# Turning q and k of batches 1 to 3 by one crossbar DMA per batch in place of TensorE transposes

## The chip, the cores and the metric

The kernel runs on one core of a Trainium2 chip. The metric is device time in microseconds. Three timed runs of the kernel before gave 316.80, 317.67 and 317.11 us, a median of 317.11 us. One profiled execution took 317.23 us; its span, from the first to the last instruction in the trace, is 315.4 us. All readings of the trace are in microseconds from the start of that span.

## The reference, cut to what matters

Attention over 4 batches, 8 heads, 768 positions and head size 64 with a block mask, followed by a gated feed-forward over the 3072 tokens:

```
scores = (q @ k.T) / 8                      # per batch and head, 768 x 768
mask   = block mask of 24 x 24 blocks of 32 # window, first/last blocks, 3 random ones per row
attn   = softmax(where(mask, scores, -1e9))
x      = (attn @ v), heads side by side     # 3072 x 512
gate   = sigmoid(x @ w_gate)                # 512 -> 1536
out    = (gate * (x @ w_val)) @ w_out       # 1536 -> 512, float32
```

For the score product TensorE needs q and k with the head dimension on the partitions. They come from memory with the positions on the partitions, so each has to be transposed. That transposition is what the change moves.

## The kernel before, in words

**Units.** The work is cut into 12 units of 256 query positions, three per batch: units 0 to 2 are batch 0, units 3 to 5 batch 1, units 6 to 8 batch 2, units 9 to 11 batch 3. A unit has four head pairs, and a pair has three steps of 256 key positions each. A step is a group of 8 score matmuls (line 381), one exponential of 128x1024 on ScalarE (line 391) and one product with the mask on VectorE (line 397). The pair's products are then multiplied with v by 24 matmuls (line 420), normed on VectorE (lines 430 and 432) and transposed by two TensorE instructions (line 441).

**Feed-forward.** Each unit's feed-forward runs under the attention of the next units: 12 groups of 8 matmuls (line 505, with the tanh at line 516 and the gating at line 521), then two output groups of 12 matmuls (line 544), whose results are copied to `ysb` (four buffers) and stored by a DMA on SP's queue (line 562). The output groups of unit n stand in unit n + 2.

**Preps.** `prep` (line 318) turns q or k of one head pair of one batch. VectorE copies two heads side by side into `pr` (line 326), TensorE transposes six 128x128 blocks of it into a PSUM bank (line 335), and ScalarE or VectorE copies the bank to `qT` or `kT` (lines 222 and 224). There are 8 such preps for each of batches 1, 2 and 3. `vcopy` (line 359) copies v of a pair beside a column of ones. `q16`, `k16`, `v16`, `vex`, `qT` and `kT` each have two buffers, one for even and one for odd batches.

**Loads.** All loads go through POOL's queue in program order (line 175 for q, k and v, lines 185 and 190 for the weights) and convert float32 to float16. Those of batch 1 stand at the end of the start-up list; those of batches 2 and 3 wait until the buffer of the batch before the last has been copied (`later`, line 592).

**Order.** `Plan` (line 54) simulates the engines with a table of costs, hands each free engine the first ready task in program order, and the resulting order is then written out, engine by engine. On the chip every engine runs its own list in that order, and an instruction that waits holds up all that stands behind it on its engine.

Of the kernel before, what the change touches and what calls it, by code (L numbers as in the profile page):

```python
# [13 lines left out]
f16 = mybir.dt.float16  # L14
# [6 lines left out]
B, H, S, D = 4, 8, 768, 64  # L21
BLK = 32
NB = S // BLK
NT = S // 128
NP = H // 2
# [6 lines left out]
NU = S // UQ  # L32
PE, ACT, DVE, DMA = "PE", "ACT", "DVE", "DMA"
# [20 lines left out]
class Plan:  # L54
# [7 lines left out]
        self.tasks = []  # L62
        self.room = {kind: [(0.0, i) for i in range(n)] for kind, n in banks.items()}

    def add(self, engines, fn, deps=(), at=0.0, take=(), free=()):
        self.tasks.append((engines, fn, list(deps), at, list(take), list(free)))
        return len(self.tasks) - 1

    def run(self):
        n = len(self.tasks)  # L70
        left = [len(set(t[2])) for t in self.tasks]
        after = [[] for _ in range(n)]
        for i, t in enumerate(self.tasks):
            for d in set(t[2]):
                after[d].append(i)
        ready = sorted(i for i in range(n) if not left[i])
        busy = {PE: 0.0, ACT: 0.0, DVE: 0.0, DMA: 0.0}
        events = [(0.0, -1)] + [(t[3], -1) for t in self.tasks if t[3] > 0]
        heapq.heapify(events)
        order, end = [], 0.0  # L80
        while events:
            now, i = heapq.heappop(events)
            if i >= 0:
                for bank in self.tasks[i][5]:
                    self.room[bank.kind].append((now, bank.slot))
                for j in after[i]:
                    left[j] -= 1
                    if not left[j]:
                        bisect.insort(ready, j)
            if events and events[0][0] <= now:  # L90
                continue
            for eng in busy:
                if busy[eng] > now:
                    continue
                for j in ready:
                    engines, fn, _, at, take, _ = self.tasks[j]
# [12 lines left out]
                    heapq.heappush(events, (now + cost, -1))  # L109
                    heapq.heappush(events, (now + cost + self.LAG[eng], j))  # L110
# [10 lines left out]
def kernel(  # L121
# [11 lines left out]
    nc = tc.nc  # L133
# [6 lines left out]
            name=nc.get_next_instruction_name(), act_func_set_id=_set_id  # L140
# [11 lines left out]
    sing = ctx.enter_context(tc.tile_pool(name="sing", bufs=1))  # L152
# [12 lines left out]
    wo = sing.tile([128, NF, DM], f16)  # L165
    q16 = [sing.tile([128, H, NT, D], f16, name=f"q16_{r}") for r in range(2)]
    k16 = [sing.tile([128, H, NT, D], f16, name=f"k16_{r}") for r in range(2)]
    v16 = [sing.tile([128, H, NT, D], f16, name=f"v16_{r}") for r in range(2)]
    vex = [sing.tile([128, H, NT, D + 1], f16, name=f"vex{r}") for r in range(2)]
    qT = [sing.tile([128, NP, S], f16, name=f"qT{r}") for r in range(2)]  # L170
    kT = [sing.tile([128, NP, S], f16, name=f"kT{r}") for r in range(2)]


    def load_heads(dst, src, b, h0, h1, t0=0, t1=NT):
        nc.gpsimd.dma_start(  # L175
            dst[b % 2][:, h0:h1, t0:t1, :],
            src[b, h0:h1].rearrange("h (p t) d -> p h t d", t=NT)[:, :, t0:t1, :],
        )
# [79 lines left out]
    land = {}  # L258
# [59 lines left out]
    def prep(src, dst, b, p, t0, t1, deps, at):  # L318
# [35 lines left out]
            [(DVE, 0.14 + 0.07 * n), (ACT, 0.18 + 0.1 * n)], evac, [c] + deps, free=[bank]  # L354
        )

    def vcopy(b, p, deps, at):
        def go(eng):
            nc.vector.tensor_copy(
                vex[b % 2][:, 2 * p : 2 * p + 2, :, 0:D],  # L360
                v16[b % 2][:, 2 * p : 2 * p + 2, :, :],
            )

        a = plan.add([(DVE, 0.36)], go, loaded[b] + deps, at=at)
        copies[b].append(a)
        return a
# [37 lines left out]
    class Pair:  # L404
# [34 lines left out]
        def turn(self, eng):  # L439
            for s in range(2):  # L440
                nc.tensor.transpose(  # L441
                    m16(self.bank2.slot)[:, s * 128 : (s + 1) * 128],
                    self.x16[:, s, :, :],
                    ident,
                )
# [25 lines left out]
    def scores(run):  # L471


        def mm(eng):
            for pr, st in run:
                st.qk()

        deps = [x for pr, st in run for x in (kdone[pr.b, pr.p], qdone[pr.b, pr.p, pr.u])]
# [96 lines left out]
    xTs = [[] for _ in units]  # L575
    xdone = [[] for _ in units]
    ffn = [Ffn(n) for n in range(len(units))]
    masks, kdone, qdone, vdone, read = {}, {}, {}, {}, {}
    preps, valued, turned = deque(), deque(), deque()

    def prep_k(b, p, at=0.0):
        kdone[b, p] = prep(k16, kT, b, p, 0, NT, read.get(("qk", b - 2, p), []), at)

    def prep_q(b, p, at=0.0, t0=0, t1=NT):
        d_ = prep(q16, qT, b, p, t0, t1, read.get(("qk", b - 2, p), []), at)
        for u in range(t0 // 2, t1 // 2):
            qdone[b, p, u] = d_

    def prep_v(b, p, at=0.0):
        vdone[b, p] = vcopy(b, p, read.get(("pv", b - 2, p), []), at)  # L590

    def later(b):
        if b > 1:

            def load(eng):
                for src, dst in ((k, k16), (q, q16), (v, v16)):
                    load_heads(dst, src, b, 0, H)
# [109 lines left out]
```

## Time and profile before

| | |
|---|---|
| median of three runs | 317.11 us (316.80 to 317.67) |
| profiled execution | 317.23 us |
| its span | 315.4 us |
| TensorE busy | 299.3 us of the span |
| VectorE busy | 214.1 us |
| ScalarE busy | 214.1 us |
| transposes of preps (line 335) | 192 instructions, 17.1 us |

A timeline row gives the start, the duration, the engine, the line, the operation, the output and inputs with their shapes, and how many instructions were merged into the row; behind it, in brackets, stands the idle time before it and what ended that. A row by windows gives a stretch, its length, and the busy time of each engine with the number of instructions.

### The profile page before, as it was taken

Reading aid. Unit: us, or ns where it says so; the run is one execution under the profiler, and the core shown is the slowest. Engines: PE = TensorE matmul, PEld = TensorE weight load, DVE = VectorE, ACT = ScalarE, POOL = GpSimd, SP = SyncE. Lnnn points to the kernel's source line nnn. Section 1 sums busy time; section 2 is a strip of 40 time slices with the busy share of each in tenths; the row PEclk is TensorE's granted clock in tenths of the full one; section 3 lists DMA queues with packets and bytes.
Section 4 is the critical chain, followed back from the end, with each engine's and each line's share of the span. In section 5 each row is a group of like instructions: output and inputs, shape, how many; then the busy total and the mean of one; then the engine's idle time right before and its main releaser. Section 6 shows DMA issues by size and latency. Waiting matters only on the chain.

```text
span 315.4 us, 8130 instructions
## 1 busy us (share of the span) xinstructions
PE 299.3 (95%) x3470; PEld 217.6 (69%) x3470; DVE 214.1 (68%) x510; ACT 214.1 (68%) x344; POOL 25.9 (8%) x37
## 2 busy tenths in 40 slices
PE   2978999869999999999999999999999999999995
PEld 1355786658587688588588588588588588588682
DVE  4779878478577587688576578678577476577140
ACT  4679877737777677677778677677678678676341
POOL 8944301200000000000000000000000000000000
PEclk9999999999999999999999999999999999999999
DMA  7999999999100100100010100000000000100101
GB/s 101 179 201 203 207 204 204 234 202 150 67 3 2 69 2 1 69 2 2 33 36 2 59 10 3 35 33 2 35 35 1 35 35 3 55 14 2 67 2 67
DMA packets 23215, 21.03 MB, mean 67 GB/s; under 512 B 2164, under 2 KB 20108, under 8 KB 23180
## 3 DMA queue, kind: packets, MB, share of 16 engines
q0 software_dynamic: 19472, 14.16, 29.7%
q1 hardware_dynamic: 3708, 6.37, 5.5%
q8 instruction: 27, 0.44, 0.6%
q14 instruction: 8, 0.07, 0.1%
HBM read 28.39 MB, written 6.29 MB: 110 GB/s over the span
## 4 chain that ended last, share of the span: by engine, by line
PE 77%; DMA 19%; POOL 1%; DVE 1%; issue 1%; ACT 0%; POOLq 0%
PE m L505 36%; PE m L544 18%; DMA v<-in_v_dram 11%; PE m L420 10%; PE s L381 9%; DMA wo<-in_moe_w_out_dram 5%; DMA wv<-in_moe_w_val_dram 3%; PE m L335 2%; PE m L441 1%; POOL k L175 0%; POOL q L175 0%; DVE pt L397 0%; POOL v L175 0%; ACT ysb L555 0%; DVE x L432 0%
## 5 line engine op out<-in xcount | busy, mean ns | idle before, releaser
L391 ACT ACTIVATE pt<-s 128x1024 f16<-128x1024 f32 x144 | 140.2, 1027 | 7.0 <-PE s L381 6.3
L397 DVE TENSOR_TENSOR pt<-pt,mask 128x1024 f16<-128x1024 f16 x144 | 97.2, 686 | 31.0 <-ACT pt L391 30.7
L516 ACT ACTIVATE th<-m 128x256 f32<-128x256 f32 x144 | 55.1, 389 | 49.4 <-PE m L505 42.3
L505 PE MATMUL m<-xT,wg 128*128 128x256 f16 x576 | 86.7, 273 | 0.0
L505 PE MATMUL m<-xT,wv 128*128 128x256 f16 x576 | 86.4, 273 | 0.0
L521 DVE SCALAR_TENSOR_TENSOR ht<-th,m 128x256 f16<-128x256 f32 x144 | 56.9, 416 | 16.4 <-ACT th L516 15.2
L544 PE MATMUL m<-wo,ht 128*128 128x512 f16 x288 | 66.0, 379 | 0.0
L505 PEld LDWEIGHTS <-wv 128*128 128x128 f16 x576 | 56.4, 98 | 6.5
L505 PEld LDWEIGHTS <-wg 128*128 128x128 f16 x576 | 51.4, 98 | 11.1 <-issue 5.9
L420 PE MATMUL m<-vex,pt 128*128 128x65 f16 x1152 | 46.4, 196 | 3.6 <-DVE ht L521 1.8
L420 PEld LDWEIGHTS <-pt 128*128 128x128 f16 x1152 | 42.9, 99 | 8.9 <-issue 6.9
L544 PEld LDWEIGHTS <-ht 128*128 128x128 f16 x288 | 26.7, 98 | 30.5 <-issue 1.9
L381 PE MATMUL s<-qT,kT 64*128 64x256 f16 x576 | 46.9, 279 | 0.6 <-DVE qT L224 0.3
L555 ACT ACTIVATE ysb<-m 128x512 f32<-128x512 f32 x24 | 14.3, 597 | 35.2 <-PE m L544 35.2
L381 PEld LDWEIGHTS <-kT 64*128 64x128 f16 x576 | 22.0, 95 | 15.9 <-issue 8.6
L432 DVE TENSOR_TENSOR x<-m,rz 128x256 f16<-128x256 f32 x48 | 20.4, 424 | 1.7
L430 DVE RECIPROCAL rz<-m 128x4 f32<-128x4 f32 x48 | 8.7, 182 | 17.1 <-PE m L420 16.7
L335 PE MATMUL m<-ident,pr 128*128 128x128 f16 x192 | 17.1, 231 | 1.0 <-DVE kT L224 0.5
L224 DVE COPY xT<-m 128x256 f16<-128x256 f16 x32 | 9.3, 291 | 11.3 <-PE m L441 11.2
L335 PEld LDWEIGHTS <-pr 128*128 128x128 f16 x192 | 12.4, 103 | 5.5 <-issue 3.1
L441 PE MATMUL m<-ident,x 128*128 128x128 f16 x96 | 13.3, 221 | 1.5 <-DVE x L432 1.4
L441 PEld LDWEIGHTS <-x 128*128 128x128 f16 x96 | 9.0, 98 | 7.6 <-issue 1.6
(32 smaller groups left out, 87.1 us busy)
## 6 DMA issues: line engine op xcount, KB each, us to landing
out_dram<-ysb SPq DMA_DIRECT2D x24, 256.0 KB, 2.0
k<-in_k_dram POOLq DMA_DIRECT2D x3, 768.0 KB, 19.4
q<-in_q_dram POOLq DMA_DIRECT2D x3, 768.0 KB, 21.4
v<-in_v_dram POOLq DMA_DIRECT2D x3, 768.0 KB, 23.3
wg<-in_moe_w_gate_dram POOLq DMA_DIRECT2D x4, 384.0 KB, 12.6
wv<-in_moe_w_val_dram POOLq DMA_DIRECT2D x4, 384.0 KB, 13.5
wo<-in_moe_w_out_dram POOLq DMA_DIRECT2D x3, 512.0 KB, 16.5
k<-in_k_dram POOLq DMA_DIRECT2D x4, 192.0 KB, 5.5
```

Of the source, the lines that this page charges most:

```text
L335: nc.tensor.transpose(m16(bank.slot)[:, (t - t0) * 128 : (t - t0 + 1) * 128], box[0][:, t, :, :], ident,)
L381: nc.tensor.matmul(score[self.bank.slot][:, a, i, :], kT[b % 2][o : o + D, p, t * 128 : (t + 1) * 128], qT[b % 2][o : o + D, p, u * UQ : ( ...
L391: nc.scalar.activation(self.pt, score[self.bank.slot], AF.Exp, bias=0.0, scale=SCALE)
L397: nc.vector.tensor_tensor(self.pt, self.pt, m.unsqueeze(1).broadcast_to([128, 2, 2, UQ]), op=ALU.mult,)
L420: nc.tensor.matmul(self.acc[:, s, a, :], self.steps[t // 2].pt[:, a, t % 2, s * 128 : (s + 1) * 128], vex[self.b % 2][:, 2 * self.p + a, t ...
L432: nc.vector.tensor_tensor(self.x16, self.acc[:, :, :, 0:D], rz.broadcast_to([128, 2, 2, D]), op=ALU.mult,)
L441: nc.tensor.transpose(m16(self.bank2.slot)[:, s * 128 : (s + 1) * 128], self.x16[:, s, :, :], ident,)
L505: nc.tensor.matmul(pg[:, i, :], w[:, c, f * 128 : (f + 1) * 128], xTs[self.n][0][:, c, :], start=(c == 0), stop=(c == 3),)
L516: nc.scalar.activation(th, spare[bank.slot][:, 0:UQ], AF.Tanh, bias=0.0, scale=0.5)
L521: nc.vector.scalar_tensor_tensor(self.ht[:, f, :], in0=box[0], scalar=1.0, in1=spare[bank.slot][:, UQ : 2 * UQ], op0=ALU.add, op1=ALU.mult,)
L544: nc.tensor.matmul(spare[bank.slot], self.ht[:, f, s * 128 : (s + 1) * 128], wo[:, f, :], start=(f == 0), stop=(f == NF - 1),)
L555: nc.scalar.activation(ysb, spare[bank.slot], AF.Copy, bias=0.0, scale=0.5)
```

## The change

For batch 0 nothing changes. For batch 1 q and k are loaded as before, VectorE copies the head pairs side by side into two new tiles, `kp` and `qp`, which hold all four pairs of a batch (`pair_up`), and one transposing DMA on SP's queue writes all of `kT`, another one all of `qT` (`xbar`). For batches 2 and 3 the load itself writes the head pairs side by side: eight DMAs for k and eight for q, one per head, each with rows of 64 elements (`pair_load`). The transposing DMAs follow on SP's queue. `kp` and `qp` have one buffer each, so the load of batch 2 waits for the transposing DMAs of batch 1, and that of batch 3 for those of batch 2. A task can now have a delay of its own in `Plan` (`lag`), 10.0 for a transposing DMA and 55.0 for such a load; these are numbers of the order table.

```diff
+    qp = sing.tile([128, NP, NT, 2, D], f16, name="qp")
+    kp = sing.tile([128, NP, NT, 2, D], f16, name="kp")
...
+    def pair_up(src, dst, b, p, deps, at):
+        def go(eng):
+            nc.vector.tensor_copy(
+                dst[:, p, :, :, :],
+                src[b % 2][:, 2 * p : 2 * p + 2, :, :].rearrange("a h t d -> a t h d"),
+            )
+        return plan.add([(DVE, 0.36)], go, deps, at=at)
+
+    def xbar(src, dst, b, deps):
+        def go(eng):
+            nc.sync.dma_start_transpose(
+                dst[b % 2].rearrange("a p (t n) -> a (p t) n", n=128),
+                src.rearrange("a p t h d -> a (p t h d)"),
+            )
+        return plan.add([(DMA, 0.01)], go, deps, lag=10.0)
...
+    def pair_load(dst, src, b):
+        for p in range(NP):
+            for a in range(2):
+                nc.gpsimd.dma_start(
+                    dst[:, p, :, a, :],
+                    src[b, 2 * p + a].rearrange("(n t) d -> n t d", t=NT),
+                )
+
     def later(b):
-        if b > 1:
+        kr = [x for p in range(NP) for x in read.get(("qk", b - 2, p), [])]
+        if b == 1:
+            # for k, then q: four pair_up, then one xbar
...
+        else:
             def load(eng):
-                for src, dst in ((k, k16), (q, q16), (v, v16)):
-                    load_heads(dst, src, b, 0, H)
-            loaded[b].append(plan.add([(DMA, 0.01)], load, copies[b - 2]))
-        for p in range(NP):
-            for nm, fn in (("k", prep_k), ("q", prep_q), ("v", prep_v)):
-                preps.append(
-                    lambda fn=fn, p=p, at=land[nm, "next"] if b == 1 else 0.0: fn(b, p, at)
-                )
+                pair_load(kp, k, b)
+                pair_load(qp, q, b)
+                load_heads(v16, v, b, 0, H)
+            ld = plan.add(
+                [(DMA, 0.01)],
+                load,
+                [turned_b["k", b - 1], turned_b["q", b - 1]] + copies[b - 2],
+                lag=55.0,
+            )
+            loaded[b].append(ld)
+            turned_b["k", b] = xbar(kp, kT, b, [ld] + kr)
+            turned_b["q", b] = xbar(qp, qT, b, [ld] + kr)
...
+        for p in range(0, NP, 2):
+            at = land["v", "next"] if b == 1 else 0.0
+            preps.append(lambda p=p, at=at: [prep_v(b, p + i, at) for i in range(2)])
```

The change also moves instructions. On VectorE, in unit 2, where batch 1 is prepared (`k_1` and `q_1` are batch 1; `k_0`, `q_0` and `v_0` at this place are batch 2), there stood before, with the copies for batch 2 at the end:

```order
L326 COPY pr<-q_1_74 128x768
L359 COPY vex_80<-v_1_78 128x12x64 x2
L397 TENSOR_TENSOR pt<-pt,mask 128x1024
L224 COPY xT<-m_125 128x256
L359 COPY vex_80<-v_1_78 128x12x64 x2
L326 COPY pr<-k_0_75 128x768
L430 RECIPROCAL rz<-m_122 128x4
L432 TENSOR_TENSOR x_977<-m_122,rz 128x256
L397 TENSOR_TENSOR pt<-pt,mask 128x1024
L326 COPY pr<-q_0_73 128x768
L397 TENSOR_TENSOR pt<-pt,mask 128x1024
```

Now the same place reads as follows (line 422 is the mask product, 455 and 457 the norm, 384 the copy of v, 364 the new pairing copy):

```order
L364 COPY kp<-k_1_76 128x768 x4
L548 SCALAR_TENSOR_TENSOR ht<-th,m_124 128x256
L422 TENSOR_TENSOR pt<-pt,mask 128x1024 x2
L455 RECIPROCAL rz<-m_125 128x4
L457 TENSOR_TENSOR x_832<-m_125,rz 128x256
L364 COPY qp<-q_1_74 128x768 x4
L422 TENSOR_TENSOR pt<-pt,mask 128x1024 x2
L227 COPY xT<-m_127 128x256
L384 COPY vex_82<-v_1_80 128x12x64 x3
L455 RECIPROCAL rz<-m_125 128x4
L457 TENSOR_TENSOR x_922<-m_125,rz 128x256
L422 TENSOR_TENSOR pt<-pt,mask 128x1024 x2
```

The four k copies and the four q copies stand together, and no copy for batch 2 stands in unit 2 any more; the four copies of batch 2's v come 60 mask products into the program, those of batch 3's v 95 into it.

SP's queue had four small loads and then the 24 stores of the output. Now the transposing DMAs stand between the stores (`kT_86` and `qT_84` are the buffers of batches 1 and 3, `kT_85` and `qT_83` those of batch 2):

```order
L375 DMA_TRANSPOSE kT_86<-kp 128x24x128
L589 DMA out_dram<-ysb 128x512
L375 DMA_TRANSPOSE qT_84<-qp 128x24x128
L589 DMA out_dram<-ysb 128x512 x5
L375 DMA_TRANSPOSE kT_85<-kp 128x24x128
L375 DMA_TRANSPOSE qT_83<-qp 128x24x128
L589 DMA out_dram<-ysb 128x512 x6
L375 DMA_TRANSPOSE kT_86<-kp 128x24x128
L375 DMA_TRANSPOSE qT_84<-qp 128x24x128
L589 DMA out_dram<-ysb 128x512 x12
```

The q transposition of batch 1 stands behind the first store of unit 0, those of batch 2 behind the second store of unit 2, and those of batch 3 behind the second store of unit 5.

On POOL's queue the end of the list was one DMA each for k, q and v of batches 1, 2 and 3. For batches 2 and 3 there now stands:

```order
L622 DMA kp<-in_k_dram 128x6x64 x8
L622 DMA qp<-in_q_dram 128x6x64 x8
L178 DMA v_0_79<-in_v_dram 128x8x384
L622 DMA kp<-in_k_dram 128x6x64 x8
L622 DMA qp<-in_q_dram 128x6x64 x8
L178 DMA v_1_80<-in_v_dram 128x8x384
```

The load of v now stands behind sixteen smaller DMAs. On TensorE the 24 groups of six transposes of batches 1 to 3 are gone, and the other groups keep their places but for a neighbour here and there; the first score group of units 3, 6 and 9 is the first to read what a transposing DMA wrote.

More of the change, by code (lines that the diff above doesn't have):

```diff
@@ L63, in __init__, with add @@
         self.room = {kind: [(0.0, i) for i in range(n)] for kind, n in banks.items()}
-    def add(self, engines, fn, deps=(), at=0.0, take=(), free=()):
-        self.tasks.append((engines, fn, list(deps), at, list(take), list(free)))
+    def add(self, engines, fn, deps=(), at=0.0, take=(), free=(), lag=None):
+        self.tasks.append((engines, fn, list(deps), at, list(take), list(free), lag))
         return len(self.tasks) - 1
@@ L95, in run @@
                 for j in ready:
-                    engines, fn, _, at, take, _ = self.tasks[j]
+                    engines, fn, _, at, take, _, lag = self.tasks[j]
                     cost = dict(engines).get(eng)
@@ L109, in run @@
                     heapq.heappush(events, (now + cost, -1))
-                    heapq.heappush(events, (now + cost + self.LAG[eng], j))
+                    lag = self.LAG[eng] if lag is None else lag
+                    heapq.heappush(events, (now + cost + lag, j))
                     order.append((eng, fn))
@@ L476, in mm @@
                 st.qk()
-        deps = [x for pr, st in run for x in (kdone[pr.b, pr.p], qdone[pr.b, pr.p, pr.u])]
+        deps = [
+            x for pr, st in run for x in kdone[pr.b, pr.p] + qdone[pr.b, pr.p, pr.u]
+        ]
         a = plan.add([(PE, 0.1 + 0.22 * len(run))], mm, deps, take=[st.bank for pr, st in run])
@@ L577 @@
     ffn = [Ffn(n) for n in range(len(units))]
-    masks, kdone, qdone, vdone, read = {}, {}, {}, {}, {}
+    masks, kdone, qdone, vdone, read, turned_b = {}, {}, {}, {}, {}, {}
     preps, valued, turned = deque(), deque(), deque()
     def prep_k(b, p, at=0.0):
-        kdone[b, p] = prep(k16, kT, b, p, 0, NT, read.get(("qk", b - 2, p), []), at)
+        kdone[b, p] = [prep(k16, kT, b, p, 0, NT, [], at)]
     def prep_q(b, p, at=0.0, t0=0, t1=NT):
-        d_ = prep(q16, qT, b, p, t0, t1, read.get(("qk", b - 2, p), []), at)
+        d_ = [prep(q16, qT, b, p, t0, t1, [], at)]
         for u in range(t0 // 2, t1 // 2):
```

22 lines of the change are left out of this document (added).

## The prediction

> **What bounds the kernel now.** I read the page's busy times and slices first, then its chain, then TensorE's share of the preps.
>
> ```profile
> PE 299.3 (95%) x3470; PEld 217.6 (69%) x3470; DVE 214.1 (68%) x510; ACT 214.1 (68%) x344; POOL 25.9 (8%) x37
> ...
> PE   2978999869999999999999999999999999999995
> ...
> DMA  7999999999100100100010100000000000100101
> ...
> PE 77%; DMA 19%; POOL 1%; DVE 1%; issue 1%; ACT 0%; POOLq 0%
> ...
> L335 PE MATMUL m<-ident,pr 128*128 128x128 f16 x192 | 17.1, 231 | 1.0 <-DVE kT L224 0.5 <-DVE pr L326 0.4
> ```
>
> From about the tenth slice on TensorE is busy in nine tenths of each slice or more; before that the DMA engines are full, and the eighth and ninth slices (55 to 71 us) show TensorE at 8 and 6 tenths. So two things can be gained: TensorE work in the long dense stretch, and idle time around 60 us. VectorE and ScalarE at 68% bound nothing.
>
> A matmul's recorded 231 ns overlaps its neighbours, so it is no price. The price is what a prep adds to a unit. The view by windows, cut at the first score group of units 3 to 11 and limited to line 335, shows it (length, then TensorE busy and count; six are one prep):
>
> ```profile
> 76.54:99.96 23.42, 0.50 (x6) 0.38 (x6) 1.00 0.09 27
> 99.96:124.06 24.10, 1.52 (x18) 1.05 (x18) 1.00 0.07 23
> 124.06:148.50 24.44, 2.01 (x24) 1.43 (x24) 1.00 0.07 23
> 148.50:171.92 23.42, 0.50 (x6) 0.38 (x6) 1.00 0.07 24
> 171.92:196.02 24.10, 1.52 (x18) 1.05 (x18) 1.00 0.06 23
> 196.02:220.45 24.43, 2.01 (x24) 1.43 (x24) 1.00 0.06 23
> 220.45:243.54 23.09, 0.00 (x0) 0.00 (x0) 1.00 0.07 24
> 243.54:266.63 23.09, 0.00 (x0) 0.00 (x0) 1.00 0.07 25
> ```
>
> A unit without a prep takes 23.09 us; one prep makes it 23.42, three 24.10, four 24.44. That is 0.34 us per prep, very regular, hence TensorE time and nothing else.
>
> The idle time shows in the timeline of TensorE and VectorE, and in one row of the unrestricted windows:
>
> ```profile
> 48.36:76.54 28.18, 24.82 (x295) 18.62 (x292) 21.03 (x55) 17.67 (x29) 2.63 (x3) 1.00 1.30 211
> ...
> 48.36 0.83 PE L335 MATMUL m<-ident,pr 128*128 128x128 f16 x12
> ...
> 63.99 0.93 PE L420 MATMUL m<-vex,pt 128*128 128x65 f16 x24 [1.85 <-DVE ht L521]
> ...
> 68.07 0.27 PE L441 MATMUL m<-ident,x 128*128 128x128 f16 x2 [1.40 <-DVE x L432]
> ```
>
> ```profile
> 62.65 0.36 DVE L326 COPY pr<-q 128x768 f16<-128x768 f16 x1 [3.03 <-DMA q<-in_q_dram]
> ...
> 66.51 0.36 DVE L359 COPY vex<-v 128x768 f16<-128x768 f16 x1 [1.91 <-DMA v<-in_v_dram]
> ```
>
> VectorE stands at the copies of batch 2's q and v, which have not landed yet; mask products and gatings are queued behind them, and TensorE runs dry behind those: 28.18 - 24.82 = 3.36 us idle between the first prep of batch 1 (48.36) and the first score group of batch 1 (76.54).
>
> **The change part by part.**
>
> *Preps of batches 2 and 3, taken off TensorE.* The six windows from 76.54 to 220.45 hold 16 preps and last 143.91 us; six clean ones last 6 x 23.09 = 138.54. Gain: 5.37 us.
>
> *Preps of batch 1.* All 8 lie between 48.36 and 76.54. At 5.37 / 16 = 0.336 us each: 2.69 us.
>
> *The stall.* In unit 2 no copy waits for batch 2 any more, so what TensorE waited for at 63.99 and 68.07 is gone: 3.36 us. VectorE's next copies in the queue are those of batch 1's v, which the trace shows without a wait at 55.00 (row below). I count the whole 3.36.
>
> *VectorE and ScalarE* lose the copies into and out of the transposes. Since a clean unit already runs at TensorE's pace, that is worth nothing.
>
> *The new waits: when the transposing DMAs of batch 1 begin.*
>
> ```profile
> 47.21 0.62 DVE L326 COPY pr<-k 128x768 f16<-128x768 f16 x2
> ...
> 51.05 0.62 DVE L326 COPY pr<-q 128x768 f16<-128x768 f16 x2
> ...
> 55.00 0.63 DVE L359 COPY vex<-v 128x768 f16<-128x768 f16 x2
> ...
> 51.82 0.60 ACT L555 ACTIVATE ysb<-m 128x512 f32<-128x512 f32 x1 [1.72 <-PE m L544]
> ```
>
> k of batch 1 is copied at 47.21 with no wait ahead of it. Four copies in a row, two of which take 0.62, end at about 48.5, and the k transposition is issued. The q copies follow two mask products and a norm, near 51; they end about 52. The q transposition also stands behind the first store of unit 0, whose `ysb` (51.82 to 52.42) comes some 0.7 us sooner without the two preps ahead of it. So q is issued near 52.
>
> *When they are needed.* The first score group of unit 3 comes at 76.54 - 3.36 - 2.69 = 70.5. On one queue the second follows the first, so with T for one transposition both are there at 48.5 + 2T. The cover is 22.0 us and holds up to T = 11.0; beyond, TensorE waits 2T - 22.0.
>
> *What T is.* No row shows a transposing DMA. The nearest:
>
> ```profile
> q0 software_dynamic: 19472, 14.16, 29.7%
> q1 hardware_dynamic: 3708, 6.37, 5.5%
> ...
> out_dram<-ysb SPq DMA_DIRECT2D x24, 256.0 KB, 2.0
> ...
> ident<-bb_ident SPq DMA_DIRECT2D x1, 32.0 KB, 1.6
> ```
>
> It moves 768 KB in 24 x 128 = 3072 rows of 256 B. From below: SP's queue moved 6.37 MB in 5.5% of 315.4 us, 367 GB/s; 0.786 MB take 2.1 us, with the landing of the smallest row (1.6) 3.7 us. From above by packets: 3708 packets in 16 x 17.3 us are 75 ns each; 192 rows per engine make 14.4, with the landing 16.0 us. Far above: `ident` is one 128x128 block of rows of 256 B and lands in 1.6 us; were each of the 24 blocks such a transfer of its own, one behind the other, 38.4 us. It is one DMA with many rows, so the packet rows are nearest; between 3.7 and 16.0 I take 10. Then batch 1's last transposition is there at 68.5, 2 us ahead of its need, and costs nothing. The 38.4 stays for a rival.
>
> *The loads of batches 2 and 3.* Their 16 DMAs have 12,288 rows of 128 B in place of 2048 of 768 B.
>
> ```profile
> L175 POOL DMA_DIRECT2D k<-in_k_dram x7 | 5.7, 819 | 18.6 <-DVE qT L224 15.9 <-DVE pt L397 1.3 <-POOLq L691 0.8
> ...
> 40.00:50.00 10.00, 10.00 (x136) 8.06 (x132) 7.73 (x20) 8.55 (x15) 0.00 (x0) 1.00 1.31 204
> ...
> 108.05 0.33 SPq L562 DMA_DIRECT2D out_dram<-ysb  x1
> ...
> 180.01 0.33 SPq L562 DMA_DIRECT2D out_dram<-ysb  x1
> ...
> 122.98 0.68 DVE L397 TENSOR_TENSOR pt<-pt,mask 128x1024 f16<-128x1024 f16 x1
> ...
> 193.47 0.68 DVE L397 TENSOR_TENSOR pt<-pt,mask 128x1024 f16<-128x1024 f16 x1
> ```
>
> By bytes (1.57 MB at 204 GB/s) k and q take 7.7 us; by packets (POOL's queue spent 77 ns on each of its 19,472) 59 us; issuing 17 DMAs at 0.82 is 14 us. I take the middle of the ends, 33 us, and 3.9 for v. Batch 2: k starts when its buffer is free (58.5), v lands near 95. VectorE copies that v after 60 mask products, at 122.98 before, so at 122.98 - 6.05 - 4 x 0.336 = 115.6: 20 us of cover. Its transpositions stand behind the second store of unit 2 (108.05 before, near 101), end near 121, and are needed by unit 6 at 148.50 - 6.05 - 8 x 0.336 = 139.8: 18 us. Batch 3: `kp` is free at 111, v lands near 148; its copy stands after 95 mask products (193.47, less 9.7: 183.7). Its transpositions stand behind the second store of unit 5 (180.01, near 171), end near 191, needed by unit 9 at 209.0: 18 us. Stores queued behind a waiting transposition have four buffers, and the next one comes a whole unit later. So the loads cost nothing, and if all that cover is gone the price is in the rivals.
>
> **Sum.** 5.37 + 2.69 + 3.36 = 11.42 us. The profiled execution took 317.23 with a span of 315.4; less 11.42, span 304.0 and time 305.8. The median shown is 317.11, so execution and median agree to 0.12.
>
> **The rivals.**
>
> *Slower: the crossbar is slow.* If the 24 blocks go one by one, T is near `ident`'s 1.6 per block. Batch 1 waits 2T - 22.0; batches 2 and 3, from 101 to 139.8 and from 171 to 209, each wait 2T - 38. At T = 16.7 the first wait eats the whole gain, and from there on the change loses; T = 20 gives 305.8 + 18 + 2 + 2 = 328, T = 38.4 gives 305.8 + 54.8 + 38.8 + 38.8 = 438. For it: nothing in the trace excludes such a price. Against it: all other rows show the queues overlapping packets on 16 engines. Here the Trainium skill speaks against the change: "VectorE: DVE Perf Modes", section "The three transpose paths", gives 1309 ns for a 128x128 block by DMA against 390 ns on TensorE, and its rules advise TensorE where a PSUM destination will do. The trace disagrees on TensorE (0.336 us for six blocks, 56 ns each); for the DMA no run here shows it. By its figure T would be an estimated 31.4 us, and the time about 396 us.
>
> *Faster, but with a wait at unit 3.* T between 11.0 and 16.7: TensorE waits 0 to 11 us once, batches 2 and 3 are still covered. T = 14 gives 305.8 + 6 = 312.
>
> *The stall only moves.* Batch 1's v is loading until near 55 while the k transposition shares its DMA engines. If v comes several us later, VectorE stands at its copies as it stands at 62.65 now, and the 3.36 is not won: 309.2. Against it: TensorE has about 3 us of queued work that needs nothing behind those copies.
>
> *The small rows are slow.* At the full 77 ns per row batch 2's v lands at 58.5 + 59 + 3.9 = 121.4, 6 us after its copy is due, and batch 3's about when due: 305.8 + 6 = 312. The Trainium skill, "DMA: Bandwidth & Descriptors", section "Specifications", says that transfers under 512 B fall below line rate; no row here is as small as 128 B, and it gives no price.
>
> **How the numbers follow.** Forecast 0.56, wait at unit 3 0.17, slow crossbar 0.14, stall moved 0.08, slow rows 0.05. The forecast's own range is 303 to 308: the low end prices each of the 24 preps by the time that the chain of waits gives one (row below), 24 x 0.44 + 3.36 = 13.9 off; the high end leaves 2 us of wait.
>
> ```profile
> 141.01 0.44 PE m L335 x6
> ```
>
> The range to hold 8 in 10 goes up through the second, fourth and fifth case to T = 16.5: 303 to 317. What a measurement can tell from no change is 0.3%, about 1 us. Faster than that: the forecast and the three mild cases but for the last stretch of the second, 0.83; within it 0.03; slower 0.14.
>
> **What would show it.** Right: line 335 left with 48 transposes; every unit from 3 to 11 at 23.1 us; no idle time of TensorE over 1 us between 55 and 75; the transposing DMAs landing within 11 us, and no wait of a score group for one. Wrong: first score groups of units 3, 6 or 9 waiting for `kT` or `qT` (slow crossbar), VectorE waiting at copies of v, or units that stay above 23.4 with no prep in them.

## The result, and the profile after

The changed kernel takes 306.72 us, the median of four runs (305.60 to 307.56), against 316.96 us (316.80 to 317.67) for the kernel before in the same comparison: ratio 0.9671, 95% interval 0.9633 to 0.9708. (Ratios leave out a run that is over 1.5% above the fastest of its kernel.) The prediction was 305.8. The profiled execution took 306.27 us with a span of 304.5 (predicted 304.0).

The page of the kernel after, in the lines that were shown of the kernel before:

```profile
PE 291.4 (96%) x3326; PEld 209.6 (69%) x3326; DVE 200.9 (66%) x474; ACT 210.7 (69%) x340; POOL 48.5 (16%) x65
...
PE   3978999999999999999999999999999999999994
...
DMA  7999999999500699930100580100100100100101
...
q0 software_dynamic: 40400, 14.16, 40.8%
q1 hardware_dynamic: 22332, 11.09, 15.0%
...
PE 93%; ACT 2%; DMA 1%; DVE 1%; issue 1%; POOL 1%; POOLq 0%
```

TensorE has 144 instructions less, and the 8 and 6 of the eighth and ninth slices are 9 and 9 now. The share of DMA in the chain has gone from 19% to 1%. The loads and transposing DMAs of batches 2 and 3 stand as separate bursts (the digits over 1 behind the tenth slice), with low slices between them.

The same windows of the kernel after, unit 2 first, then units 3, 5, 6, 8 and 9, then from unit 11 to the end (length; TensorE, weight load, VectorE, ScalarE, POOL busy; granted clock; DMA share; GB/s):

```profile
47.23:70.33 23.10, 23.10 (x274) 16.89 (x274) 18.37 (x47) 17.06 (x28) 12.21 (x16) 1.00 1.59 184
70.33:93.42 23.09, 23.09 (x273) 16.97 (x273) 15.44 (x36) 16.80 (x27) 1.70 (x3) 1.00 0.58 75
...
116.51:139.61 23.10, 23.10 (x274) 16.98 (x274) 16.74 (x39) 17.08 (x28) 7.41 (x9) 1.00 1.04 104
139.61:162.70 23.09, 23.09 (x273) 16.96 (x274) 15.44 (x36) 16.80 (x27) 0.00 (x0) 1.00 0.07 24
...
185.79:208.89 23.10, 23.10 (x274) 16.88 (x274) 16.02 (x38) 17.06 (x28) 0.00 (x0) 1.00 0.07 24
208.89:231.98 23.09, 23.09 (x273) 16.97 (x273) 15.44 (x36) 16.80 (x27) 0.00 (x0) 1.00 0.07 24
...
255.07:304.50 49.43, 45.00 (x445) 32.06 (x444) 22.33 (x53) 24.18 (x44) 0.00 (x0) 0.98 0.09 33
```

Length and TensorE's busy time are the same number in every row but the last, which is the end of the program: no stall is left. Units 3, 6 and 9 begin at 70.33, 139.61 and 208.89 (predicted 70.5, 139.8 and 209.0).

The transposing DMAs of the kernel after, in SP's timeline around unit 2 (start, time for which the DMA held SP's queue):

```profile
48.60 6.18 SPq L375 DMA_TRANSPOSE kT<-kp  x1
54.83 0.58 SPq L589 DMA_DIRECT2D out_dram<-ysb  x1
55.46 3.85 SPq L375 DMA_TRANSPOSE qT<-qp  x1
```

And by tile, `kT` first and then `qT`, all three batches:

```profile
DMA to landing us min/median/max: 6.1/7.2/8.2
...
DMA to landing us min/median/max: 5.7/7.1/7.8
```

The longest of each, 8.2 and 7.8, are batch 1's. So k is there at 48.60 + 8.2 = 56.8 and q at 55.46 + 7.8 = 63.3, 7.1 us ahead of unit 3. SP is held for less time than a transposition takes, and the q one was issued 1.3 us before the k one had landed.

### The profile page after: what moved, and what is told of

Read it like the earlier page. It is cut to its first block, busy times and chain, and to the rows that moved or that the text cites. A ratio compares the mean times of both kernels' runs of the same rounds, so it can differ in the third digit from the quotient of the medians.

```text
span 304.5 us, 7858 instructions
## 1 busy us (share of the span) xinstructions
PE 291.4 (96%) x3326; PEld 209.6 (69%) x3326; DVE 200.9 (66%) x474; ACT 210.7 (69%) x340; POOL 48.5 (16%) x65
## 3 DMA queue, kind: packets, MB, share of 16 engines
q1 hardware_dynamic: 22332, 11.09, 15.0%
## 4 chain that ended last, share of the span: by engine, by line
PE 93%; ACT 2%; DMA 1%; DVE 1%; issue 1%; POOL 1%; POOLq 0%
PE m L532 42%; PE m L571 21%; PE s L406 13%; PE m L445 13%; PE m L466 2%; DMA v<-in_v_dram 1%; ACT pt L416 1%; PE m L303 1%; PE m L338 1%; ACT mask L225 1%; DVE pt L422 0%; DVE kT L227 0%; POOL k L178 0%; POOL q L178 0%; ACT ysb L582 0%
## 5 line engine op out<-in xcount | busy, mean ns | idle before, releaser
L548 DVE SCALAR_TENSOR_TENSOR ht<-th,m 128x256 f16<-128x256 f32 x144 | 57.3, 418 | 16.4 <-ACT th L543 14.8
L622 POOL DMA_DIRECT2D kp<-in_k_dram x16 | 13.0, 822 | 64.1 <-DMA kT<-kp 37.9
L622 POOL DMA_DIRECT2D qp<-in_q_dram x16 | 13.1, 827 | 0.7 <-DVE pt L422 0.4
```

The lines of the kernel that those rows point to most:

```text
L548: nc.vector.scalar_tensor_tensor(self.ht[:, f, :], in0=box[0], scalar=1.0, in1=spare[bank.slot][:, UQ : 2 * UQ], op0=ALU.add, op1=ALU.mult,)
L622: nc.gpsimd.dma_start(dst[:, p, :, a, :], src[b, 2 * p + a].rearrange("(n t) d -> n t d", t=NT),)
```

## Experiments

The theory is the prediction's sum: three terms that add, with the transposing DMAs hidden. The rivals that the result does not exclude by itself are that one term is larger than told and another smaller, and that the cover was there by luck. Four questions follow: do the terms stand alone (the first three), how far does the cover reach (the fourth), what sets the time of a transposition and of the loads (the fifth to tenth), and can it be beaten (the last two).

### The stall alone

In the kernel before, the order table's cost of a load is raised, so that the copies of batch 2 are put later. All transposes stay on TensorE.

```diff
-    LAG = {PE: 0.25, ACT: 0.06, DVE: 0.06, DMA: 16.0}
+    LAG = {PE: 0.25, ACT: 0.06, DVE: 0.06, DMA: 40.0}
```

> The kernel before with one number of the order table changed (the delay that the table gives a load, 40 in place of 16), so that no copy of batch 2 stands in unit 2 any more; all transposes stay on TensorE. Theory (the change gains 3.36 us by the stall and 8.06 us by TensorE time, each on its own): the idle time at 62 to 68 us goes, first score group of unit 3 at 73.2, time 317.0 - 3.4 = 313.6. Rival (the stall is only paid elsewhere, the whole gain is TensorE time): 317.0.

Measured: 313.09 us (312.22 to 313.92), ratio 0.9865 (0.9831 to 0.9899); span 312.1. Its windows, from the first prep of batch 1 to 73.00, just ahead of unit 3, and units 3 to 8:

```profile
48.36:73.00 24.64, 24.64 (x306) 18.97 (x303) 20.24 (x51) 18.10 (x29) 2.63 (x3) 1.00 1.30 213
73.23:217.15 143.92, 143.92 (x1730) 107.12 (x1730) 105.61 (x247) 102.39 (x164) 0.00 (x0) 1.00 0.10 28
```

TensorE is busy for the whole of the first stretch, and unit 3 begins 3.31 us sooner than before (73.23 against 76.54). Units 3 to 8 last 143.92, as before (143.91). The span lost 3.3 us. The stall is its own term, it was worth what the prediction gave it (3.36), and it could be had without the crossbar.

### Batches 2 and 3 by crossbar, batch 1 on TensorE

```diff
         if b == 1:
-            for nm, src, dst, dT, done in (
-                ("k", k16, kp, kT, kdone),
-                ("q", q16, qp, qT, qdone),
-            ):
...
+            for p in range(NP):
+                for nm, fn in (("k", prep_k), ("q", prep_q)):
...
+                        fn(b, p, land[nm, "next"])
```

> The change for batches 2 and 3 alone; batch 1 keeps its preps on TensorE. Theory: first score group of unit 3 at 73.2 (stall gone, 8 preps still there), units 3 to 8 at 23.1 each, time 306.7 + 2.7 = 309.4. Rival (batch 1's preps cost nothing, since TensorE has to wait in the start-up anyway): 306.7.

Measured: 309.40 us (308.94 to 309.75), ratio 0.9746 (0.9711 to 0.9780). Unit 2, with the 8 preps of batch 1 in it, and unit 3:

```profile
48.09:73.87 25.78, 25.78 (x322) 19.66 (x322) 20.50 (x51) 19.46 (x32) 9.43 (x11) 1.00 1.43 143
73.87:96.96 23.09, 23.09 (x273) 16.97 (x273) 15.41 (x36) 16.80 (x27) 0.00 (x0) 1.00 0.07 24
```

25.78 - 23.10 = 2.68 us for 8 preps (predicted 2.69), and no idle time. Unit 3 begins at 73.87, 0.7 us later than was expected; unit 2 had begun 0.86 us later than in the change. The kernel is 2.7 us behind the change.

### Batch 1 by crossbar, batches 2 and 3 as before

The copies of batch 2 were kept late as in the first experiment, so that only the preps of batch 1 and the stall should be gone.

```diff
-    LAG = {PE: 0.25, ACT: 0.06, DVE: 0.06, DMA: 16.0}
+    LAG = {PE: 0.25, ACT: 0.06, DVE: 0.06, DMA: 40.0}
...
-                pair_load(kp, k, b)
-                pair_load(qp, q, b)
-                load_heads(v16, v, b, 0, H)
+                for src, dst in ((k, k16), (q, q16), (v, v16)):
+                    load_heads(dst, src, b, 0, H)
...
+                for fn in (prep_k, prep_q, prep_v):
+                    preps.append(lambda fn=fn, p=p: fn(b, p, 0.0))
```

> The change for batch 1 alone; batches 2 and 3 keep their loads and their preps on TensorE, with their copies standing late in the order (delay 40 in the table). Theory: first score group of unit 3 at 70.3 as in the change, the 16 preps of units 3 to 8 cost 5.4 us, time 306.7 + 5.4 = 312.1. Rival (the loads of small rows and the transposing DMAs of batches 2 and 3 cost something in the change): nearer to 311 or below.

Measured: 330.57 us (329.79 to 331.04), ratio 1.0414 (1.0381 to 1.0447). That is a miss by 18 us, and on the other side of the kernel before. SP's timeline of this kernel, its landing rows by tile (`kT`, then `qT`), TensorE's timeline, and the window of unit 3:

```profile
47.86 11.76 SPq L377 DMA_TRANSPOSE kT<-kp  x1
60.30 17.61 SPq L377 DMA_TRANSPOSE qT<-qp  x1
```

```profile
DMA to landing us min/median/max: 22.0/22.0/22.0
...
DMA to landing us min/median/max: 27.0/27.0/27.0
```

```profile
87.45 1.03 PE L408 MATMUL s<-qT,kT 64*128 64x256 f16 x8 [17.79 <-DMA qT<-qp]
```

```profile
87.45:112.85 25.40, 25.40 (x274) 18.00 (x274) 16.07 (x39) 16.84 (x27) 0.00 (x0) 0.90 0.07 24
```

The same two DMAs took 22.0 and 27.0 us in place of 8.2 and 7.8, and the first score group of unit 3 waited 17.79. The k one was issued at nearly the same time as in the change (47.86 against 48.60), the q one 4.8 us later (60.30 against 55.46), because the first held SP's queue for longer. What differs beside them is that the loads of batches 2 and 3 write into `k16`, `q16` and `v16`. Those of batch 2 were issued from 32.86 to 37.09 already, those of batch 3 from 48.77 on; the six landed one after another from 59.6 to 88.7, while the transpositions ran. These are the three of batch 3 in POOL's timeline:

```profile
48.77 0.88 POOL L178 DMA_DIRECT2D k<-in_k_dram  x1 [10.81 <-DVE pt L424]
51.53 0.87 POOL L178 DMA_DIRECT2D q<-in_q_dram  x1 [1.88 <-DVE qp L364]
58.71 0.87 POOL L178 DMA_DIRECT2D v<-in_v_dram  x1 [6.30 <-DVE vex L386]
```

In the change the loads of k write into `kp` and those of q into `qp`, and each has to wait until the transposition of the batch before has read that tile. In the trace of the change the first load of batch 2's k is issued at 57.41, 0.6 us after the k transposition has landed (56.8), and the first of q at 63.91, after the q one has (63.3); the first load of batch 3's k waits 37.9 us for the k transposition of batch 2. So the hold is not complete: batch 2's k is loaded beside the q transposition of batch 1.

Two theories remained: the loads take from the transposition something that both need (contention), or a transposition into this `kT` is slow for a reason of its own. The fifth, seventh and eighth runs below go on from here.

### How far the cover reaches

In the change, batch 1's transposing DMAs are issued three times; the first two write into `k16[0]` and `q16[0]`, which nobody reads by then.

```diff
+            if b == 1:
+                for s16 in (k16[0], q16[0]):
+                    nc.sync.dma_start_transpose(
+                        s16.rearrange("a h t d -> a (h t d)").rearrange(
+                            "a (x n) -> a x n", n=128
+                        ),
+                        src.rearrange("a p t h d -> a (p t h d)"),
+                    )
             nc.sync.dma_start_transpose(
```

> The change with each transposing DMA of batch 1 issued three times, the first two into buffers that nothing reads any more, so that the last q transposition lands later; nothing else is added. Theory (two transpositions had 22 us of cover and took 14.6 of it; an extra one costs 4 to 6 us of SP's queue): the last q transposition lands near 81, the first score group of unit 3 waits about 11 us for it, time 306.7 + 11 = 317 to 318. Rival (the score groups have other work ahead or the DMAs overlap, so that there is much more cover): within 2 us of 306.7.

Measured: 320.31 us (319.49 to 323.31), ratio 1.0110 (1.0052 to 1.0168). TensorE's timeline, and the windows of the idle stretch, of the stretch with the lower clock, of unit 3 and of unit 4:

```profile
82.29 1.04 PE L414 MATMUL s<-qT,kT 64*128 64x256 f16 x8 [11.50 <-DMA qT<-qp]
```

```profile
70.80:82.20 11.40, 0.00 (x0) 0.00 (x0) 0.60 (x2) 0.38 (x1) 1.91 (x3) 0.62 1.66 204
73.50:87.10 13.60, 4.81 (x38) 2.72 (x39) 1.80 (x4) 1.94 (x2) 4.39 (x6) 0.50 1.48 154
82.29:107.60 25.31, 25.31 (x274) 17.98 (x274) 14.74 (x34) 16.47 (x26) 7.36 (x9) 0.90 0.80 85
107.60:130.69 23.09, 23.09 (x274) 16.95 (x274) 15.42 (x36) 16.79 (x27) 6.49 (x8) 1.00 0.82 116
```

Four more transpositions use up the cover and put 11.50 us of wait at unit 3, as expected: where the cover ends, the whole excess comes through. But the time went up by more. Unit 3 lasts 25.31 us, 2.22 more than unit 4, at a mean granted clock of 0.90: the clock stood at 0.5 from 73.5 to 87.1, still 4.8 us after TensorE had begun again. 4.8 us at half speed are 2.4 us of work, about the 2.22 seen. The Trainium skill, "TensorE: Matmul & The Clock Gate", Part 1, says that an idle window of about 3.4 us halves the clock and that a busy one restores it. The trace agrees on the halving and the return, not on the times: here the clock fell 2.7 us after the idle time began and came back 4.8 us after its end.

### Contention or not: the loads held back

The third experiment again, with one addition: POOL sets one element per partition of `kp` and `qp` ahead of batch 2's loads (nobody reads it), so that these wait until both transpositions have read their tiles. Batch 3's loads stand behind them in POOL's queue and are held back too; all six are issued from 61.30 to 65.63.

```diff
+                if b == 2:
+                    for t in (kp, qp):
+                        nc.gpsimd.memset(t[:, 0, 0, 0, 0:1], 0.0)
                 for src, dst in ((k, k16), (q, q16), (v, v16)):
...
+            held = [turned_b["k", 1], turned_b["q", 1]]
```

> The kernel of e3_batch_1 (batch 1 by the crossbar, batches 2 and 3 on TensorE) with one thing added: before the load of batch 2 POOL sets one element per partition of kp and one of qp, which has to wait until both transposing DMAs of batch 1 have read them; so no bulk load runs beside them. Theory (in e3_batch_1 the transpositions took 22 and 27 us because the loads of batches 2 and 3 ran on the same DMA engines): they take 7 to 9 us again, first score group of unit 3 at 70.3, time 306.7 + 5.4 = 312.1. Rival (something else in that kernel makes them slow, such as its order or the stores): again 20 us and more, time near 330.

Measured: 311.02 us (310.38 to 311.21), ratio 0.9803 (0.9770 to 0.9837). SP's timeline, and the landing rows by tile (`kT`, then `qT`):

```profile
48.66 5.65 SPq L377 DMA_TRANSPOSE kT<-kp  x1
54.99 3.90 SPq L377 DMA_TRANSPOSE qT<-qp  x1
```

```profile
DMA to landing us min/median/max: 7.7/7.7/7.7
...
DMA to landing us min/median/max: 5.8/5.8/5.8
```

The transpositions land after 7.7 and 5.8 us, and unit 3 begins at 70.39, as in the change. One edit, which keeps the loads away, takes 19.6 us off (330.57 to 311.02): 17.06 from the start of unit 3 (87.45 to 70.39), and 2.3 from its length (25.40 against 23.09), which the lower clock had added. So the loads beside the transpositions are the cause. Whether they compete for the DMA engines or for something else on the way is not told apart by any run here.

It also gives the term that the third experiment was meant for: batch 1's preps and the stall without those of batches 2 and 3. The profiled execution took 311.12 us against 317.23 before, so 6.11 us for the two terms together (predicted 2.69 + 3.36 = 6.05).

### The small rows

In the change, batches 2 and 3 are loaded in whole rows of 768 B into `k16` and `q16`, held back in the same way, and paired by VectorE as in batch 1. The order table's delay for such a load goes from 55.0 to 25.0 with it.

```diff
-                pair_load(kp, k, b)
-                pair_load(qp, q, b)
-                load_heads(v16, v, b, 0, H)
+                for t in (kp, qp):
+                    nc.gpsimd.memset(t[:, 0, 0, 0, 0:1], 0.0)
+                for src, dst in ((k, k16), (q, q16), (v, v16)):
+                    load_heads(dst, src, b, 0, H)
...
+                ups = [pair_up(src, dst, b, p, [ld, turned_b[nm, b - 1]], 0.0) for p in range(NP)]
+                turned_b[nm, b] = xbar(dst, dT, b, ups + kr)
```

> The change with batches 2 and 3 loaded whole, as before, in rows of 768 B (after the transposing DMAs of the batch before, by the same one-element settings as in e5_held) and paired by VectorE copies as batch 1 is; transposed by the crossbar. Theory (the loads of small rows are covered and VectorE has room for 16 more copies of 0.27 us): the same as the change, 306.7, within 1 us. Rival (the small rows cost something that the units do not show): faster than 305.7.

Measured: 306.83 us (306.32 to 307.29), ratio 0.9675 (0.9641 to 0.9708): no difference from the change. Nor do VectorE's 8 more copies per batch show. In the kernel after, POOL's timeline and the view of DMA issues (KB each, median from issue to landing) show how long the small rows take:

```profile
57.41 6.51 POOL L622 DMA_DIRECT2D kp<-in_k_dram  x8 [26.21 <-DVE x L457]
...
66.27 4.88 POOL L622 DMA_DIRECT2D qp<-in_q_dram  x6 [0.43 <-DVE pt L422]
71.14 0.89 POOL L178 DMA_DIRECT2D v<-in_v_dram  x1
```

```profile
kp<-in_k_dram POOLq DMA_DIRECT2D x16, 96.0 KB, 5.1
qp<-in_q_dram POOLq DMA_DIRECT2D x16, 96.0 KB, 4.5
```

The 16 DMAs of k and q are issued from 57.41 to 71.14; one lands 4.5 to 5.1 us after its issue, so they are through near 75.6, some 18 us after the first.

### The loads beside the transpositions

The opposite edit: in the change, batch 2 is loaded straight into `k16[0]` and `q16[0]`, used in the layout of `kp`, and no longer waits for batch 1's transpositions.

```diff
+    kps, qps = [other(k16[0]), kp], [other(q16[0]), qp]
...
-                pair_load(kp, k, b)
-                pair_load(qp, q, b)
+                pair_load(kps[b % 2], k, b)
+                pair_load(qps[b % 2], q, b)
...
-                [turned_b["k", b - 1], turned_b["q", b - 1]] + copies[b - 2],
+                ([turned_b["k", 1], turned_b["q", 1]] if b == 3 else []) + copies[b - 2],
```

> The change with one wait less: batch 2 is loaded into k16 and q16 of batch 0, which are free by then, in the layout of kp and qp, so its load no longer waits for the transposing DMAs of batch 1 and runs beside them. Theory (what keeps the transposition short in the change is that its loads wait, so that the DMA engines are free): both transpositions take 15 us or more, the last lands after 76, TensorE waits 6 us or more at unit 3, time 313 to 325. Rival (only large rows disturb them, or the slowness of e3_batch_1 has another cause): 306.7.

Measured: 307.00, 309.26, 311.95 and 312.05 us; ratio of the first two 0.9716 (0.9653 to 0.9779). In the profiled execution, the one of 312.05, the transpositions landed after 13.8 and 14.8 us and unit 3 waited 2.16 us. The runs lie so far apart that the same kernel was run once more.

> The kernel of e7_unheld once more, since its runs lay between 307.0 and 312.1 and only one was profiled. Theory, corrected by that run (beside loads of small rows a transposition takes about 14 us, not 8, and the last one of batch 1 lands within a few us of its need): first score group of unit 3 waits 0 to 4 us for qT, time 306 to 312. Rival (the profiled run was an exception): transpositions of 8 us.

Measured: 307.82 us (306.99 to 309.26), ratio 0.9704 (0.9659 to 0.9749). SP's timeline, the landing rows by tile (`kT` over all batches, where batch 1's is the longest; `qT`), and TensorE's timeline at unit 3:

```profile
48.42 7.90 SPq L375 DMA_TRANSPOSE kT<-kp  x1
56.99 9.38 SPq L375 DMA_TRANSPOSE qT<-qp  x1
```

```profile
DMA to landing us min/median/max: 6.2/9.9/13.5
...
DMA to landing us min/median/max: 14.7/14.7/14.7
```

```profile
71.82 0.61 PE L406 MATMUL s<-qT,kT 64*128 64x256 f16 x8 [1.60 <-DMA qT<-qp]
```

The transpositions land after 13.5 and 14.7 us and unit 3 waits 1.60. Loads beside a transposition slow it here too, but far less than in the third experiment, where these two took 22.0 and 27.0 us. The direction was right; the size expected for the first of these two runs (313 to 325 us) was not: it took the slowdown of the bulk loads for that of the small rows. The loads of the two kernels differ in more than their rows: in the third experiment the loads of batches 2 and 3 were both under way, here those of batch 2 alone. Which of the two makes the difference, and why the eight runs of this kernel lie between 306.99 and 312.05, these runs do not show.

### One DMA per head pair, one DMA per block

First all transposing DMAs of the change are cut in four, of six blocks each:

```diff
-            nc.sync.dma_start_transpose(
-                dst[b % 2].rearrange("a p (t n) -> a (p t) n", n=128),
-                src.rearrange("a p t h d -> a (p t h d)"),
-            )
+            for p in range(NP):
+                nc.sync.dma_start_transpose(
+                    dst[b % 2][:, p, :].rearrange("a (t n) -> a t n", n=128),
+                    src[:, p, :, :, :].rearrange("a t h d -> a (t h d)"),
+                )
```

> The change with each transposing DMA cut into four, one per head pair (6 blocks of 128x128 each). Theory (a DMA has a fixed part of about 2 us, the rest goes with its rows, and all of it is covered): each lands 3 to 4 us after its issue, all four of k by 58, the time stays 306.7 within 1 us. Rival (each transposing DMA has a large fixed cost on SP's queue, so that eight of them outrun the cover of 22 us): first score group of unit 3 waits, time over 309.

Measured: 305.93 us (305.32 to 306.53), ratio 0.9646 (0.9611 to 0.9681). The view by tile `kT` (ns for which one holds SP, least, median and most; landing):

```profile
L376 SPq DMA_TRANSPOSE kT<-kp x12: 1209/1276/3591, 47.5 to 175.4; - x12
...
DMA to landing us min/median/max: 3.0/4.3/8.0
```

A DMA of six blocks lands after 3.0 us at the least, 4.3 in the median, and holds SP for 1.2 to 1.3 us. Those of batch 1's k took up to 8.0 us, where 3 to 4 had been expected; the cover hides that. Then, in the change, only batch 3's are cut into single blocks, 24 for k and 24 for q:

```diff
+            if b == 3:
+                for p in range(NP):
+                    for t in range(NT):
+                        nc.sync.dma_start_transpose(
+                            dst[b % 2][:, p, t * 128 : (t + 1) * 128],
+                            src[:, p, t, :, :].rearrange("a h d -> a (h d)"),
+                        )
+                return
```

> The change with the two transposing DMAs of batch 3 cut into 24 each, one per 128x128 block; batch 3's have about 18 us of cover and no load beside them. Theory (a transposition has a fixed landing part of 2 to 3 us, and the blocks of one DMA overlap, 0.15 to 0.25 us each): a single block lands 2 to 3 us after its issue, and 48 issues of 0.4 to 1.2 us each keep SP busy for 20 to 55 us, so that unit 9 waits 0 to 20 us: time 306.7 to 327. Rival (a block costs 1.3 us wherever it stands, as the Trainium skill has it in VectorE: DVE Perf Modes, The three transpose paths; then the whole transposition of the change could not have landed in 6 us): a single block lands after 1.3 us.

Measured: 313.77 us (313.10 to 314.43), ratio 0.9896 (0.9871 to 0.9921). SP's timeline, the view by tile `kT`, and one of the waits in TensorE's timeline:

```profile
170.87 34.42 SPq L378 DMA_TRANSPOSE kT<-kp  x24
205.40 31.31 SPq L378 DMA_TRANSPOSE qT<-qp  x24
```

```profile
L378 SPq DMA_TRANSPOSE kT<-kp x24: 1093/1183/2530, 170.9 to 204.1; - x24
...
DMA to landing us min/median/max: 2.2/2.3/7.6
```

```profile
216.75 0.61 PE L414 MATMUL s<-qT,kT 64*128 64x256 f16 x4 [3.13 <-DMA qT<-qp]
```

Each single block holds SP for 1.18 us, lands after 2.3, and 48 of them occupy the queue from 170.9 to 236.7, some 1.37 us each. The q blocks come too late for unit 9. It waits 3.13 and 1.23 us for them, and the wait of 3.13 brings the granted clock down to 0.5 from 216 to 222: the 12 matmuls of the output group there take 5.27 us in place of 2.75. So a price like the slow rival's 1.3 to 1.6 us per block is real for a DMA of one block. It is a price per DMA, and not one that a DMA of 24 blocks pays 24 times: that one lands in 5.7 to 8.2 us, 0.24 to 0.34 per block. The 1309 ns of the Trainium skill ("VectorE: DVE Perf Modes", "The three transpose paths") lies near this period of single-block DMAs.

### The change again, and per pair again

> The change as it is, beside the next kernel on one chip. Theory: 306.7 as measured, within 1 us.

Measured: 305.66 us (305.36 to 306.55), ratio 0.9645 (0.9629 to 0.9661).

> The change with each transposing DMA cut into four (as e8_per_pair), timed more often and on the chip of the run above. Theory (all transpositions are covered in both): the same as the change, within 0.3%. Rival (the first score group of a unit can start sooner, or SP's shorter holds let the stores go): faster than it by 0.5 us or more.

Measured: 305.79 us (305.63 to 305.89), ratio 0.9644 (0.9631 to 0.9657). The finer DMAs bring nothing; no version tried is faster than the change by more than its runs scatter. On this chip the change itself gives 305.66, so the 0.9 us between 305.8 and the first comparison's 306.72 lies within what the runs of one kernel scatter (305.36 to 307.56).

## Why the prediction was right, and where not

**The sum** held term by term. The stall: 3.36 predicted, 3.3 of span in the first experiment. The preps of batch 1: 2.69 predicted, 2.68 in the second. The 16 preps of batches 2 and 3: predicted 5.37; the change lies 311.12 - 306.27 = 4.9 us below the kernel with only the other two terms (by medians 4.3 against the first comparison's 306.72 and 5.4 against the later 305.66, so the times alone fix this term to about 1 us). The change's units 3 to 8 last 208.89 - 70.33 = 138.56, against 143.91 before: 5.35 us. In the profiled execution the first score group of unit 11 comes 266.63 - 255.07 = 11.56 us sooner than before. Of that, 0.66 is given back behind it, at the end of the span, and without it the span would lie 0.1 below the 304.0 predicted. It lies behind TensorE's work: the last copy to `ysb` starts 11.56 us sooner too (300.11 against 311.67), but from its end to the end of the span, with one store in it, it is 3.8 us against 3.1. The other profiled runs show 2.9 to 3.3 there or 3.8 (3.8 again in the later run of the change); why stays open.

**"I take 10"** for the transposition was mis-sized: batch 1's measured 8.2 and 7.8, the later ones 5.7 to 7.2. The bounds (3.7 to 16.0) held. The rows were counted rightly, their price was not: SP's queue has 22,332 - 3,708 = 18,624 packets more than before, 3,104 for each of the six transpositions against the 3,072 told, and if the stores took as long as before they took an estimated 24 ns each (15.0% of 304.5 us less 5.5% of 315.4 us, times 16 engines), where the upper bound had 75.

**"On one queue the second follows the first"** was wrong. SP is held for 3.5 to 6.2 us of a transposition, and the next DMA may be issued before the last has landed. With the smaller T this left 7.1 us at unit 3, where 2 had been told.

**The wait at unit 3** was the rival with the next chance, and its condition was incomplete: T was treated as one unknown number, while it depends on what else is being moved. It is 5.7 to 8.3 us in the change, 13.5 and 14.7 beside all of batch 2's small-row loads, 22.0 and 27.0 beside the bulk loads. The prediction named sharing only the other way round, for batch 1's v behind the k transposition. It did not say that the single buffers of `kp` and `qp`, by making the loads wait, are what keeps the transposition short. Even so the loads of batch 2's k run beside the q transposition, from 57.41 on: it took 7.8 us there, 8.3 when the change was run again, and 5.8 in the fifth and sixth runs, which held these loads back as well. That T stayed within its cover therefore rests on a hold that the prediction did not count on, and is luck to that extent. How much hung on it differs: with another buffer for batch 2 and small rows the wait was 1.60 us and the time 307.82, still inside the forecast's 303 to 308, though other runs of that kernel went up to 312.05; with early bulk loads the kernel is 4% slower than before. The price of a wait was also too small: waits of 11.50 and 17.79 us took 2.2 and 2.3 us more through the clock, and one of 3.13 us was enough to bring the clock down.

**The slow crossbar** is refuted for this form (24 blocks in 5.7 to 8.2 us, where it gave 31 to 38). The objection drawn from the Trainium skill would hold only with a DMA per block. Even then the run with 48 single blocks lost only about 8 us on the change (313.77 against 305.66), since the score groups waited in pieces, each for the blocks that it needed (4.4 us in all), and the clock added some 2.5.

**The stall only moves** did not happen: unit 2 is 23.10 us long and TensorE busy for 23.10. VectorE's copies of batch 1's v show no wait in the kernel after:

```profile
55.02 0.89 DVE L384 COPY vex<-v 128x768 f16<-128x768 f16 x3
58.78 0.42 DVE L384 COPY vex<-v 128x768 f16<-128x768 f16 x1
```

That v was issued at 30.3 and landed 23.8 us later, near 54.1, so 0.9 us ahead of its first copy. The argument against this rival, that TensorE has queued work to cover such a wait, was not put to the test.

**The small rows** cost nothing, as predicted, with room to spare: k and q were through some 18 us after the first issue, where 33 had been taken, and the loads in whole rows gave the same time.

## What to carry to other kernels

Where TensorE is busy in all of a stretch, what it does not do there comes off the time one for one; cut the windows at one recurring instruction and read the price from units with and without the work, not from the busy time of its instructions. A transposing DMA is cheap as one large DMA, or as four, and dear as single blocks, and its time is no constant: before hiding one, look at what else will be on the DMA engines while it runs, and keep bulk loads out of that stretch, if need be by a buffer that makes them wait. The stall was cured by the order alone in one line; such a gain should be tried by itself before it is put to the credit of a larger change.

## What the runs showed of the hardware

- Loads that run beside a transposing DMA of 24 blocks slow it 1.8 to 4.7 times (7.7 and 5.8 us with the loads of batches 2 and 3 held back, 13.5 and 14.7 beside loads of 128 B rows, 22.0 and 27.0 beside bulk loads).
- A transposing DMA of 24 blocks holds the issuing queue for 3.5 to 6.2 us, up to 17.6 under that contention, while an ordinary store beside it took 0.58 us.
- The time of a transposing DMA does not grow in step with its blocks: 2.3 us for one, 3.0 at the least and 4.3 in the median for six, 5.7 to 8.2 for 24 in the change.
- After waits of 11.50 and 17.79 us TensorE ran its first 5 us at a granted clock of 0.5. That unit took 25.31 and 25.40 us in place of 23.1. The clock had fallen 2.7 and 2.3 us after the idle time began.
